# Layer 0 in half-blocks of f, late attention earlier, and two weight pairs decoded before the third block

## The chip, the cores and the metric

The kernel runs on one core of a Trainium2 chip. The metric is the device time of one execution in microseconds; lower is better. Five engines work side by side, each through a queue of its own: TensorE (PE, with its weight loads shown as PEld), VectorE (DVE), ScalarE (ACT), GpSimd (POOL) and SyncE (SP), which here issues the DMAs.

## The reference

Sliding-window attention with sink keys, then two feed-forward layers, all on 1536 tokens (2 batches of 768) of width 512:

```
scores = q @ k.T / sqrt(64)          # 8 heads of 64; keep key < 4, or 0 <= i - j < 128
x  = softmax(scores) @ v             # 1536 x 512
h  = x @ w_in                        # layer 0: 512 -> 2048
x  = (h * tanh(log(1 + exp(h)))) @ w_out      # 2048 -> 512
h  = x @ w2_in                       # layer 1
out = (h * clip(h + 3, 0, 6) / 6) @ w2_out
```

The weights arrive as 8-byte floating-point numbers.

## The kernel before

**Number format.** Every operand of a large matmul is split in two f16 parts, high and low, and a product is three matmuls (high by high, high by low, low by high). The weights are decoded on the chip: for each f, a slice of 128 of the 2048 hidden columns, SP loads two raw tiles of 512 KB (L166, L170) into one of two raw buffers, and `gen_decode` makes a 32-bit number of the two halves on DVE (L210 to L212) and splits it (ACT L222, DVE L224). Layer 1's weights are decoded in pairs of two f, because `split_pair` also forms sums and differences of the second matrix for a product with seven instead of eight multiplications (L249, L250, L260 to L268).

**Tokens.** 12 units of 128 tokens are in three blocks of four. The first eight units' attention (`First`, `first_blocks`) runs at the start. The last four (units 8 to 11, the third block) go through "late" attention: `gen_front` (keys and queries to f16, DMA transposes, scores on PE L551, minimum on DVE L558, exponent on ACT L565, split L578 and L581) and `gen_back` (values on PE L628 to L639, normalise L649, split and transpose into xt[2]). These generators yield 92 times; what lies between two yields is called a piece.

**Layer 0.** A step takes one block of 512 tokens and two f. `up` makes h with 24 matmuls of 512 columns (L737 to L739) and runs the activation: ACT L740 twice, L745, L746, L747; DVE L749 twice; ACT L753; DVE L754, which ends with the tile g. `down` multiplies g into four PSUM banks (24 matmuls, L782); it is written one step behind `up` (LAG = 1), so PE's order is up(s), down(s-1), up(s+1), down(s). There are 8 steps per block; before, the order of steps (STAGES) was all 16 f of block 0, then of block 1, then of block 2. After a block's last f, `finish` (L906, L907) takes the four banks into xt, the input of layer 1. With a span that ends before f = 16, `finish` copies the banks to SBUF on ACT instead (L897), and the later span adds them on DVE (L901).

**Layer 1** has half-blocks of 256 tokens and steps of four f (`up2`, `down2`, `finish2`).

**Side work.** `hook` is called four times a step, after each half of `up` and of `down`. At each call it takes RATES[stage] / 4 pieces of late attention and one half of a weight's decoding, the latter only up to a limit. Before, the limit was two or three f beyond what the steps so far needed (AHEAD) in the first two blocks; from the third block on it follows PAIRS, counted by step. `dec_side.until` decodes at once what the step itself needs. At the third block's first step `att_side.until` finishes late attention and `open_second` closes its buffers and opens, in their place, those for layer 1's weights.

**What sets the order.** The framework takes the instructions in the order written as their priority, and a planner with its own cost model lets each engine take the first one that it believes ready; so an instruction can stand earlier in its engine's queue than where it is written, if its data and its buffers are there. On the chip each queue then runs in the planned order.

Of the kernel before, what the change touches and what calls it, by code (L numbers as in the profile page):

```python
# [29 lines left out]
def attention_moe_moe2(  # L30
# [18 lines left out]
    KF = DFF // 128  # L49
# [21 lines left out]
    blocks = BLOCKS  # L71
    order = sum(blocks, [])
    first = blocks[0] + blocks[1]
    last = sum(blocks[2:], [])
# [81 lines left out]
    late = {}  # L156
# [312 lines left out]
    def open_second():  # L469

        p2.close()
        late["p"] = main.enter_context(tc.tile_pool(name="p_b", bufs=2))
        late["g7"] = main.enter_context(tc.tile_pool(name="g7", bufs=2 * (LAG + 1)))
        late["same"] = main.enter_context(tc.tile_pool(name="same", bufs=1))
        late["w_c"] = main.enter_context(tc.tile_pool(name="w_c", bufs=WC))
# [192 lines left out]
    def gen_units():  # L668
        assert all(u % NSB >= 2 for u in last)
        load_late(last[0])  # L670
        fr = {u: gen_front(u) for u in last}
        ahead = {u: 3 if u - 1 in last else 5 if u // NSB in {x // NSB for x in last[:n]} else 7 for n, u in enumerate(last)}
        yield from pieces(fr[last[0]], ahead[last[0]])
        for n, u in enumerate(last + [None]):
            if u is not None:
                yield from pieces(fr[u], 6)
            if n > 0:
                yield from gen_back(last[n - 1])
                yield ("unit", last[n - 1])
            if n + 1 < len(last):  # L680
                yield from pieces(fr[last[n + 1]], ahead[last[n + 1]])
            if u is not None:
                yield from pieces(fr[u], 7)
# [27 lines left out]
    att_side = Side(gen_units())  # L711
# [7 lines left out]
    def per_bank(blk):  # L719
        return 512 // (len(blocks[blk]) * 128)  # L720
# [109 lines left out]
    def down2(st, span):  # L830
        layer, blk, f = st
        g2 = gt.pop(st)
        fa, fb = span
        if f == fa:
            acc[layer, blk] = [ps_acc.tile([128, 2, 256], F32, tag="acc", name="acc") for _ in range(4)]
        a = acc[layer, blk]
        ends = f + 4 == fb
        turns = [(m, n) for m in range(2) for n in range(NP)]
        if ends:
            turns = [(m, n) for n in range(NP) for m in range(2)]  # L840
        for at, (m, n) in enumerate(turns):
            i = TURNS[n]
            g, w = g2[m][i], wt[1, 1, f // 2 + m][i]
            for x, (l_, r_) in enumerate(((g[:, 0], w[:, 0]), (g[:, 0], w[:, 1]), (g[:, 1], w[:, 0]))):

                nc.tensor.matmul(  # L846
                    a[n // 2][:, n % 2], l_, r_, start=f == fa and m == 0 and n % 2 == 0 and x == 0,
                    stop=ends and m == 1 and x == 2 and (n % 2 == 1 or n == NP - 1), skip_group_check=True,
                )
            if at % NP == NP - 1:  # L850
                hook()
        if f + 4 == fb:
            finish2(blk, {i: a[n // 2][:, n % 2] for n, i in enumerate(TURNS)}, span)
# [80 lines left out]

    steps = [((layer, j, f), (fa, fb)) for layer, j, fa, fb in STAGES for f in range(fa, fb, 2 * per_bank(j) if layer == 0 else 4)]
    budget = {"att": 0.0, "credit": 0.0, "lim": 0, "chk": False}
# [13 lines left out]

    def moe_steps():
        pend = []
        fmax = n2 = 0
        for s, (cur, span) in enumerate(steps):
            layer, j, f = cur
            fend = layer * KF + f + (2 * per_bank(j) if layer == 0 else 4)
            stage = STAGES.index((layer, j) + span)
            budget["chk"] = stage >= CHECK and not raw_t
            if f == span[0] and layer == 0 and j >= 2:
                att_side.until(("unit", blocks[j][-1]))  # L960
                open_second()
            budget["att"] = RATES[stage]
            if layer == 0 and j < 2:
                fmax = max(fmax, fend)
                budget["lim"] = 2 * min(fmax + AHEAD[stage], KF)
            else:

                budget["lim"] = 2 * (KF + 2 * PAIRS[n2])
                n2 += 1
            dec_side.until(("dec", fend - 1))  # L970
            (up if layer == 0 else up2)(cur)
            yield
            pend.append((cur, span))
            while len(pend) > LAG:
                x = pend.pop(0)
                (down if x[0][0] == 0 else down2)(*x)
        for x in pend:
            down2(*x)

    moe = moe_steps()  # L980
    first_blocks()
    p1.close()
# [187 lines left out]
NPART = 8  # L1170
TURNS = (0, 5, 4, 6, 2, 3, 1)
NATG = 2
STAGES = [(0, 0, 0, 16), (0, 1, 0, 16), (0, 2, 0, 16)]
STAGES += [(1, (j, h), fa, fa + 8) for fa in (0, 8) for j in (0, 1) for h in (0, 1)] + [(1, (2, h), 0, 16) for h in (0, 1)]
CHECK = 7
WC = 8
PAIRS = [1, 2, 3, 4, 4, 5, 6, 6, 7] + [8] * 100
LAG = 1
STB = 2
P1N = 8  # L1180
# [1 line left out]
P1V = 4  # L1182
P1D = 4
BLOCKS = [[6, 7, 0, 1], [2, 3, 4, 5], [8, 9, 10, 11]]
RATES = [2.5, 11] + [0] * 11
DPS = 1
AHEAD = [3, 2]


# [32 lines left out]
```

## Time and profile before

| | |
|---|---|
| median of 3 runs | 600.39 us (599.83 to 601.9) |
| the profiled execution | 599.53 us, span 597.7 us |
| PE busy | 579.0 us (97%) |
| DVE busy | 457.8 us (77%) |
| ACT busy | 398.4 us (67%) |
| granted TensorE clock, mean | 0.998 |

The span is the time from the first to the last instruction; the 1.8 us beyond it lie around it. An engine's idle time is the span less its busy time. The end of a matmul is modelled, so a short wait on PE shows a little smaller than it is. In the views, x is a count of instructions, and times are from the span's start.

Where the stages lie: block 0's first `up` starts at 72.4 us, beside the tail of the first attention; from 96.8 us layer 0 fills PE; block 1's first `up` starts at 161.3 us, block 2's at 264.5 us; layer 0's last `down` ends at about 361.6 us; layer 1 ends at 592.3 us.

### The profile page before, as it was taken

Reading aid. Unit: us, or ns where it says so; the run is one execution under the profiler, and the core shown is the slowest. Engines: PE = TensorE matmul, PEld = TensorE weight load, DVE = VectorE, ACT = ScalarE, POOL = GpSimd, SP = SyncE. Lnnn points to the kernel's source line nnn. Section 1 sums busy time; section 2 is a strip of 40 time slices with the busy share of each in tenths; the row PEclk is TensorE's granted clock in tenths of the full one; section 3 lists DMA queues with packets and bytes.
Section 4 is the critical chain, followed back from the end, with each engine's and each line's share of the span. In section 5 each row is a group of like instructions: output and inputs, shape, how many; then the busy total and the mean of one; then the engine's idle time right before and its main releaser. Section 6 shows DMA issues by size and latency. Waiting matters only on the chain.

```text
span 597.7 us, 11394 instructions
## 1 busy us (share of the span) xinstructions
PE 579.0 (97%) x4430; PEld 394.4 (66%) x4430; DVE 457.8 (77%) x1102; ACT 398.4 (67%) x786; POOL 24.8 (4%) x36
## 2 busy tenths in 40 slices
PE   7999999999999999899989999999999999999996
PEld 4778754444444545444434468888888888888885
DVE  5688998999365555489999999866687889874754
ACT  5998887777687776679888887434354656553532
POOL 0040010700000000000000000000000000000000
PEclk9999999999999999999999999999999999999999
DMA  9976357998334533254453442000007676400001
GB/s 179 226 163 212 101 183 199 230 261 213 96 73 74 80 60 73 47 159 141 157 192 122 163 143 71 1 1 2 1 7 249 215 263 223 142 34 1 36 1 39
DMA packets 105842, 72.24 MB, mean 121 GB/s; under 512 B 73512, under 2 KB 98088, under 8 KB 105784
## 3 DMA queue, kind: packets, MB, share of 16 engines
q1 hardware_dynamic: 105784, 71.48, 42.9%
q8 instruction: 35, 0.57, 0.4%
q14 instruction: 23, 0.19, 0.1%
HBM read 60.43 MB, written 3.15 MB: 106 GB/s over the span
## 4 chain that ended last, share of the span: by engine, by line
PE 59%; DVE 13%; ACT 12%; issue 11%; DMA 2%; POOL 2%; SPq 1%; DVEq 0%; ACTq 0%
PE acc L846 18%; PE h L806 7%; PE h L808 7%; PE h L807 7%; PE acc L782 6%; PE h L737 3%; PE h L739 2%; PE h L738 2%; DVE p L212 2%; ACT e L745 2%; ACT e L746 2%; DVE g L754 2%; ACT d L358 2%; ACT y L215 1%; PE o L393 1%
## 5 line engine op out<-in xcount | busy, mean ns | idle before, releaser
L782 PE MATMUL acc<-g,w 128*128 128x512 f16 x576 | 131.2, 379 | 5.4 <-DVE g L754 5.1
L846 PE MATMUL acc<-w,g 128*128 128x256 f16 x1008 | 113.8, 273 | 0.0
L846 PEld LDWEIGHTS <-g 128*128 128x128 f16 x1008 | 98.6, 98 | 11.4
L806 PE MATMUL h<-xt,w 128*128 128x256 f16 x384 | 104.7, 273 | 0.0
L808 PE MATMUL h<-xt,w 128*128 128x256 f16 x384 | 104.7, 273 | 0.0
L807 PE MATMUL h<-xt,w 128*128 128x256 f16 x384 | 104.7, 273 | 0.0
L782 PEld LDWEIGHTS <-w 128*128 128x128 f16 x576 | 55.3, 98 | 71.6 <-issue 7.0
L737 PE MATMUL h<-xt,w 128*128 128x512 f16 x192 | 72.8, 379 | 1.8 <-DVE mins L558 1.2
L739 PE MATMUL h<-xt,w 128*128 128x512 f16 x192 | 72.8, 379 | 0.0
L738 PE MATMUL h<-xt,w 128*128 128x512 f16 x192 | 72.8, 379 | 0.0
L810 ACT ACTIVATE e<-h,bias 128x512 f32<-128x512 f32 x48 | 32.5, 678 | 54.5 <-PE h L808 54.5
L811 DVE SCALAR_TENSOR_TENSOR e<-e,h 128x512 f32<-128x512 f32 x48 | 32.8, 684 | 41.8 <-ACT e L810 41.8
L823 ACT ACTIVATE g<-e 128x256 f16<-128x256 f32 x96 | 29.5, 354 | 28.8 <-DVE e L811 28.8
L823 ACT ACTIVATE g<-sm 128x512 f16<-128x512 f32 x48 | 30.2, 628 | 27.5 <-DVE sm L818 27.5
L749 DVE SCALAR_TENSOR_TENSOR e<-e,h 128x512 f32<-128x512 f32 x48 | 30.8, 683 | 16.5 <-ACT e L747 16.3
L824 DVE SCALAR_TENSOR_TENSOR g<-sm,g 128x512 f16<-128x512 f32 x48 | 33.1, 689 | 10.9 <-ACT g L823 10.8
L806 PEld LDWEIGHTS <-w 128*128 128x128 f16 x384 | 37.6, 98 | 4.6
L807 PEld LDWEIGHTS <-w 128*128 128x128 f16 x384 | 37.6, 98 | 4.5
L808 PEld LDWEIGHTS <-w 128*128 128x128 f16 x384 | 37.6, 98 | 4.3
L212 DVE SCALAR_TENSOR_TENSOR p<-raw,y 128x1024 int32<-128x1024 int32 x32 | 39.8, 1243 | 0.4
L740 ACT ACTIVATE e<-h 128x512 f32<-128x512 f32 x48 | 28.1, 588 | 16.4 <-PE h L739 16.4
L754 DVE SCALAR_TENSOR_TENSOR g<-e,g 128x1024 f16<-128x1024 f32 x24 | 29.4, 1226 | 8.3 <-ACT g L753 8.3
(172 smaller groups left out, 934.8 us busy)
## 6 DMA issues: line engine op xcount, KB each, us to landing
raw<-in_moe_w_in_dram SPq DMA_DIRECT2D x48, 512.0 KB, 4.2
raw<-in_moe_w_out_dram SPq DMA_DIRECT2D x48, 512.0 KB, 5.0
out_dram<-ob SPq DMA_DIRECT2D x12, 256.0 KB, 2.5
first<-in_k_dram SPq DMA_DIRECT2D x8, 256.0 KB, 4.8
first<-in_q_dram SPq DMA_DIRECT2D x8, 256.0 KB, 4.9
first<-in_v_dram SPq DMA_DIRECT2D x8, 256.0 KB, 3.1
nk<-in_k_dram SPq DMA_DIRECT2D x5, 256.0 KB, 5.1
nv<-in_v_dram SPq DMA_DIRECT2D x5, 256.0 KB
```

Source lines behind the costliest of these rows:

```text
L212: nc.vector.scalar_tensor_tensor(out=p, in0=t[:, :, 1], scalar=3, in1=y, op0=ALU.logical_shift_left, op1=ALU.bitwise_xor)
L737: nc.tensor.matmul(o, wh, x[:, 0, c, :], start=c == 0, stop=False)
L738: nc.tensor.matmul(o, wh, x[:, 1, c, :], start=False, stop=False)
L739: nc.tensor.matmul(o, wl, x[:, 0, c, :], start=False, stop=c == KD - 1)
L754: nc.vector.scalar_tensor_tensor(out=gl, in0=e, scalar=sc, in1=gh, op0=ALU.mult, op1=ALU.subtract)
L782: nc.tensor.matmul(o, l_, r_, start=first and m == 0 and x == 0, stop=last and end and x == 2, skip_group_check=True)
L806: nc.tensor.matmul(o, wh, x[:, 0, c, :], start=c == 0, stop=False)
L807: nc.tensor.matmul(o, wh, x[:, 1, c, :], start=False, stop=False)
L808: nc.tensor.matmul(o, wl, x[:, 0, c, :], start=False, stop=c == KD - 1)
L823: nc.scalar.activation(out=g[:, 0, d_], in_=src, func=AF.Copy, scale=sc)
L824: nc.vector.scalar_tensor_tensor(out=g[:, 1, d_], in0=src, scalar=sc, in1=g[:, 0, d_], op0=ALU.mult, op1=ALU.subtract)
L846: nc.tensor.matmul(a[n // 2][:, n % 2], l_, r_, start=f == fa and m == 0 and n % 2 == 0 and x == 0, stop=ends and m == 1 and x == 2 and (n ...
```

## The change

Blocks 0 and 1 of layer 0 are done in halves of f: block 0 with f 0 to 7, block 1 with f 0 to 7, block 0 with f 8 to 15, block 1 with f 8 to 15, then block 2 as before. So there are 16 steps in the first two blocks as before, in another order, and two more stage borders. The decoding limit of layer 0 is a list by step (DECS): after four steps 9 f, then one f a step. The rate of late attention rises from 2.5 to 8 pieces a step in the first four steps and is 9.5 in the next eight (before: 11 from the ninth step on). `open_second` is called at the first step at whose beginning late attention is all written, not at the third block's first step; from then on PAIRS counts, and it has four more entries at the front (1, 1, 2, 2), then 2, 3, 3, 4, 4, 5, 6, 6 in the third block (before: 1, 2, 3, 4, 4, 5, 6, 6). CHECK moves with the two more stages and names the same stage as before.

```diff
     def moe_steps():
         pend = []
-        fmax = n2 = 0
+        n2 = 0
         for s, (cur, span) in enumerate(steps):
             layer, j, f = cur
             fend = layer * KF + f + (2 * per_bank(j) if layer == 0 else 4)
             stage = STAGES.index((layer, j) + span)
             budget["chk"] = stage >= CHECK and not raw_t
-            if f == span[0] and layer == 0 and j >= 2:
-                att_side.until(("unit", blocks[j][-1]))
+            unit = ("unit", last[-1])
+            if layer == 0 and j >= 2:
+                att_side.until(unit)
+            if "w_c" not in late and unit in att_side.done:
                 open_second()
             budget["att"] = RATES[stage]
-            if layer == 0 and j < 2:
-                fmax = max(fmax, fend)
-                budget["lim"] = 2 * min(fmax + AHEAD[stage], KF)
+            if "w_c" not in late:
+                budget["lim"] = 2 * DECS[s]
             else:
 
                 budget["lim"] = 2 * (KF + 2 * PAIRS[n2])
...
-STAGES = [(0, 0, 0, 16), (0, 1, 0, 16), (0, 2, 0, 16)]
+STAGES = [(0, j, fa, fa + 8) for fa in (0, 8) for j in (0, 1)] + [(0, 2, 0, 16)]
 STAGES += [(1, (j, h), fa, fa + 8) for fa in (0, 8) for j in (0, 1) for h in (0, 1)] + [(1, (2, h), 0, 16) for h in (0, 1)]
-CHECK = 7
+CHECK = 9
 WC = 8
-PAIRS = [1, 2, 3, 4, 4, 5, 6, 6, 7] + [8] * 100
+PAIRS = [1, 1, 2, 2, 2, 3, 3, 4, 4, 5, 6, 6, 7] + [8] * 100
...
-RATES = [2.5, 11] + [0] * 11
+RATES = [8, 9.5, 9.5, 14] + [0] * 11
 DPS = 1
-AHEAD = [3, 2]
+DECS = [4, 6, 8, 9, 10, 11, 12, 13, 14, 15, 16, 16, 16, 16, 16, 16]
```

## Rows read from the trace of the kernel before

**Rows 1.** The page, its first part: busy us (share of the span) and instructions.
```profile
PE 579.0 (97%) x4430; PEld 394.4 (66%) x4430; DVE 457.8 (77%) x1102; ACT 398.4 (67%) x786; POOL 24.8 (4%) x36
```

**Rows 2.** Busy time by stage: stretch, length, each engine's busy us, clock, DMA.
```profile
96.77:161.29 64.52, 62.97 (x311) 28.35 (x310) 52.24 (x77) 48.31 (x65) 11.53 (x11) 1.00 0.80 206
161.29:264.52 103.23, 99.75 (x762) 49.76 (x761) 59.41 (x133) 76.06 (x137) 0.30 (x1) 1.00 0.40 82
264.52:361.61 97.09, 94.16 (x458) 44.57 (x456) 92.56 (x148) 82.49 (x124) 0.00 (x0) 1.00 0.42 141
361.61:592.26 230.65, 230.65 (x2113) 206.55 (x2111) 172.32 (x479) 111.23 (x256) 0.00 (x0) 1.00 0.24 81
```

**Rows 3.** Waits of PE from 96 to 362 us: total us, times, longest.
```profile
PE acc L782 <- DVE g L754: 5.1, 6, 1.4
PE h L737 <- DVE mins L558: 1.2, 1, 1.2
PE o L628 <- DMA atg<-ag: 0.7, 1, 0.7
PE h L737 <- DVE e L749: 0.6, 1, 0.6
```

**Rows 4.** Groups by line and shape, the activation: count | busy us, mean ns.
```profile
L740 ACT ACTIVATE e<-h 128x512 f32<-128x512 f32 x48 | 28.1, 588 | 16.4 <-PE h L739 16.4
L745 ACT ACTIVATE e<-e,one 128x1024 f32<-128x1024 f32 x24 | 27.5, 1146 | 0.6
L747 ACT ACTIVATE e<-e 128x1024 f32<-128x1024 f32 x24 | 25.2, 1049 | 0.4
L749 DVE SCALAR_TENSOR_TENSOR e<-e,h 128x512 f32<-128x512 f32 x48 | 30.8, 683 | 16.5 <-ACT e L747 16.3
L754 DVE SCALAR_TENSOR_TENSOR g<-e,g 128x1024 f16<-128x1024 f32 x24 | 29.4, 1226 | 8.3 <-ACT g L753 8.3
```

**Rows 5.** The same view, decoding of the weights.
```profile
L210 DVE TENSOR_SCALAR y<-raw 128x1024 int16<-128x1024 int16 x32 | 24.3, 759 | 4.6 <-DMA raw<-in_moe_w_out_dram 2.5 <-ACT y L215 1.9
L212 DVE SCALAR_TENSOR_TENSOR p<-raw,y 128x1024 int32<-128x1024 int32 x32 | 39.8, 1243 | 0.4
L224 DVE SCALAR_TENSOR_TENSOR w<-p,w 128x1024 f16<-128x1024 f32 x16 | 19.7, 1230 | 0.7 <-ACT w L222 0.5
L250 DVE SCALAR_TENSOR_TENSOR w<-p,w 128x512 f16<-128x512 f32 x16 | 11.1, 692 | 0.8 <-ACT w L249 0.8
L261 DVE TENSOR_TENSOR t<-p,t 128x256 f32<-128x256 f32 x8 | 3.4, 430 | 0.1
L268 DVE SCALAR_TENSOR_TENSOR w<-t,w 128x1024 f16<-128x1024 f32 x8 | 9.8, 1228 | 1.6 <-ACT w L267 1.6
```

**Rows 6.** The same view, late attention.
```profile
L565 ACT ACTIVATE d<-d,mins 128x272 f32<-128x272 f32 x32 | 16.3, 510 | 9.4 <-DVE mins L558 9.4
L558 DVE CUSTOM_DVE_ANT_0 d<-s,m_all 128x272 f32<-128x272 f32 x32 | 12.6, 437 | 4.7 <-PE s L551 4.7
L503 DVE SCALAR_TENSOR_TENSOR k<-nk,k 128x512 f16<-128x512 f32 x5 | 3.4, 685 | 0.1
L502 ACT ACTIVATE k<-nk 128x512 f16<-128x512 f32 x5 | 3.1, 627 | 3.0 <-DMA nk<-in_k_dram 2.1 <-DMA kt<-k 0.7
```

**Rows 7.** The same view, a PSUM bank copied on ACT, one read on DVE.
```profile
L371 ACT ACTIVATE at<-tp 128x512 f32<-128x512 f32 x22 | 12.4, 596 | 0.7 <-PE tp L369 0.7
L413 DVE TENSOR_TENSOR xf<-o,rib 128x512 f32<-128x512 f32 x8 | 5.5, 689 | 4.9 <-PE o L393 3.8 <-ACT d L358 1.2
```

**Rows 8.** Busy time by step (columns as in Rows 2), three steps of block 0.
```profile
117.66:128.59 10.93, 10.93 (x62) 4.97 (x60) 10.16 (x15) 7.91 (x10) 0.05 (x1) 1.00 1.17 299
128.59:139.52 10.93, 10.93 (x62) 4.95 (x61) 9.77 (x17) 8.40 (x15) 0.00 (x0) 1.00 0.96 236
150.93:161.29 10.36, 10.36 (x50) 4.67 (x49) 3.42 (x5) 6.74 (x8) 0.00 (x0) 1.00 0.36 115
```

**Rows 9.** DVE's timeline at the end of late attention: start us, us, what.
```profile
252.19 0.68 DVE L649 TENSOR_TENSOR xf<-o,ri 128x512 f32<-128x512 f32 x1
252.91 1.22 DVE L212 SCALAR_TENSOR_TENSOR p<-raw,y 128x1024 int32<-128x1024 int32 x1
```

## The prediction

> **What bounds the kernel now.** I read the page's first part first: PE is busy for 579.0 of 597.7 us [rows 1], so 18.7 us is all that could be won without taking matmuls away, and the change takes none away. Then the busy time by stage, to see where those idle microseconds lie [rows 2]: 64.52 - 62.97 = 1.55 us in block 0 (from the point where layer 0 has PE to itself), 103.23 - 99.75 = 3.48 in block 1, 97.09 - 94.16 = 2.93 in block 2, and nothing in layer 1, where PE is busy for 230.65 of 230.65 us. The change reorders layer 0 and moves work inside it; of its idle time there are 7.96 us, 1.3% of the span, and the rest of the 18.7 us lies in the start and the very end. Next, who ends those waits [rows 3]: 5.1 us in six waits are `down` waiting for the tile g that DVE L754 makes last in a step's activation; two waits (0.6 and 1.2 us) are `up` waiting for a PSUM bank that DVE still reads (L749, L558); one (0.7 us) is the last unit's values waiting for a DMA transpose. So PE sets the time, and where it stops, DVE is late in eight waits out of nine. The loads of DVE tell why [rows 2]: busy for 52.24 of 64.52 us in block 0 (81%, although its last step needs only 3.42 of 10.36 us; two earlier ones are at 93% and 89% [rows 8]), 59.41 of 103.23 (58%) in block 1, 92.56 of 97.09 (95%) in block 2. The work is there, but badly spread: full, half empty, full.
>
> **The change part by part.** One step of layer 0 takes 10.36 us of PE when nothing else is on it [rows 8]. Its activation takes 2 x 0.683 + 1.226 = 2.6 us of DVE and 2 x 0.588 + 2 x 1.146 + 2 x 1.049 = 5.6 us of ACT (L746 is of L745's form, L753 of L747's) [rows 4]. To decode one f of layer 0 takes 2 x 0.759 + 1.243 + 1.230 = 4.0 us of DVE (L211 is like L210) and some 1.05 of ACT, one pass of L747's size [rows 4, 5]. A pair of layer 1 takes 2 x (2 x 0.759 + 1.243 + 0.692) + 5 x 0.43 + 1.228 + 0.692 = 11.0 us of DVE: L210 to L212 and L250 twice, four sums like L261, and the split L268 of 1024 columns, with one of 512 and one of 256 that I take at L250's and L261's prices [rows 5]. Late attention on DVE is 32 x 0.437 + 8 x 1.226 (L581, of L754's form) + 23 conversions x 0.685 = 39.6, some 42 us with its small instructions; on ACT 32 x 0.510 + 8 x 1.05 + 19 x 0.627 = 36.6, some 39 us with the small ones [rows 4, 6]. Over 92 pieces that is 0.46 us of DVE and 0.42 of ACT each. On PE: block 1's stretch has eight steps, 99.75 - 82.9 = 16.9 us more than the steps alone, for about 84 pieces [rows 2, 8], so 0.2 us a piece.
>
> *Steps 2 and 3 of block 0* (the first two lie in the tail of the first attention and decode the same as before). Before, each of steps 2 to 6 had 2 f and 2.5 pieces on DVE: 2.6 + 8.0 + 1.2 = 11.8 us against 10.9 of PE, five steps in a row, and DVE ran full [rows 8]; this is block 0's 1.55 us. After: step 2 has 2 f and 8 pieces, 2.6 + 8.0 + 3.7 = 14.3 against 10.4 + 1.6 = 12.0; step 3 one f, 10.3 against 12.0. One step of 2.3 us too much and then relief, in place of five of 0.9. I keep 0.8 us, half of what is there.
>
> *Steps 4 to 10* now hold one f and 9 to 10 pieces each: DVE 2.6 + 4.0 + 4.4 = 11.0, ACT 5.6 + 1.05 + 4.0 = 10.6, PE 10.4 + 1.9 = 12.3. Both helpers at about 90%, where block 1 before had DVE at 58% and ACT at 76.06 of 103.23 (74%) [rows 2]. The new border at step 4 adds four copies of a PSUM bank on ACT, 4 x 0.596 = 2.4 us, as does the one at step 8 [rows 7]. Before, the only border inside attention was the one from block 0 to 1, with the same four on ACT and four on DVE, and there stood the two waits for PSUM banks, 0.6 + 1.2 = 1.8 us [rows 3]. At none of the new borders does DVE take part while attention runs, and pieces come at 9.5 and not 11 a step: I take half, 0.9 us; the ends are 0 and one such pair of waits at each border, 3.6.
>
> *The tail of attention*, steps 10 and 11: the last unit has nothing behind it to fill the time in which its weights are transposed. Before that cost the 0.7 us of the DMA wait, and a wait for g of about the same length beside it [rows 3]; nothing in the change touches this. I keep 1.6 us.
>
> *Opening the second buffers.* 4 pieces in step 1, 8 in steps 2 and 3 each, and 38 in the four steps of each of the next two stages make 96 by step 11; 92 are needed. So `open_second` comes at step 12 and not 16. DVE then starts layer 1's decoding as soon as the last unit is normalised: before, L212 followed L649 by 0.7 us [rows 9], twelve microseconds ahead of where it is written. The same should happen some 35 to 40 us earlier. Steps 12 to 15 take two pairs, 22 us of DVE, beside 4 x 2.6 and the additions at step 12 (four of 0.689 and four of `finish`, 5.5 us [rows 7]): 38 of 41.4 us, with step 11 almost empty before them.
>
> *Block 2* loses these two pairs and gains at its head block 1's additions: 92.56 - 22 + 2.8 = 73 of some 95 us, 77% in place of 95% [rows 2]. Its 2.93 us of waits were DVE's; I leave 0.9, one wait, for the steps that still take a whole pair.
>
> *The added work as a whole* is eight copies (4.8 us of ACT) and eight additions (5.5 us of DVE) [rows 7]; I cost it at nothing, since PE works beside it; fully exposed it would be 10.3, and I take 0 as the nearer end because the one border seen cost 1.8 with eight such instructions. Freeing PSUM banks at a border can't gain, as layer 0 uses the same four banks. `down` matmuls don't change in number. On SP's queue the transposes of attention now stand between loads of raw weights, which block 1 had not; a transpose that waits for its data holds the loads behind it. With two raw buffers and one f a step a load has about a step's time (12 us) in reserve, so 0 here, at most the 2.5 us that DVE waited for raw tiles in three places before [rows 5].
>
> Sum of what is left: 0.8 + 0.9 + 1.6 + 0.9 = 4.2 us, in place of 7.96: 3.8 us less. From the profiled execution's 599.53 us this gives 595.7; the median of the runs shown lies 0.86 above it, so 596.6 us for a median.
>
> **A rule weighed.** The six waits for L754 are the last link of a chain that changes between ACT and DVE [rows 3, 4]. The Trainium skill says of this, on its page PSUM — Partial Sum Buffer, section Engine vs sequencer instructions, that the queues of ScalarE and VectorE are strictly first in, first out. By that rule a piece that the planner put ahead of the activation holds it for its whole length, at 90% load too; what it would make of steps 2 to 10 is the first rival below.
>
> **The rivals.** *The waits move* into steps 2 to 10. For it: there ACT and DVE are both at about 90%, while block 2 before had DVE at 95% and ACT at 85% and lost 2.93 us in eight steps [rows 2]; the same rate over nine steps is 3.3, with the tail's 1.6, step 2's 0.8, the borders' 0.9 and block 2's 0.9 together 7.5: 600 us, no change. Against: attention's deadline is step 16, so the planner can let pieces slip.
>
> *All that can go goes*: only the tail's 1.6 us stay, 6.4 less, 594.0 us. For it: two steps at 93% and 89% of DVE, with scores in them, had no wait on PE at all [rows 8]. Against: no stage with attention was free of waits.
>
> *Slower: PSUM runs out.* `up` takes two of the four banks, a round of scores two more, and both are freed by DVE (L749, L558). With DVE at 90% rather than 58% the release comes later; the point where it decides is a DVE queue more than half an `up`, 2.6 us, behind PE. Then each of the 16 rounds of scores costs what the cheaper of the two such waits did, 0.6 us: 9.6, less the 1.8 already paid, plus the 1.6 at the tail unchanged, while blocks 0 and 2 gain 0.75 + 2.0: 600.4 + 7.8 - 2.8 = 605.4 us. For it: both waits of the kind are there [rows 3]. Against: in the two steps at 117.66 and 128.59, with DVE at 93% and 89%, 24 score matmuls ran with no wait [rows 8]. The Trainium skill (Perfetto Trace Analysis, section Optimization Strategy) says that a gap repeating through a stretch can mean that the next tile finds no room in SBUF or PSUM; by that, two waits in 16 rounds speak against this rival so far.
>
> *It doesn't do what it says*: attention isn't written by step 12, because a piece was miscounted. Then block 2 keeps its pairs, and only block 0's 0.75 us is won against the borders' copies: 599.7 us. The count above has four pieces to spare.
>
> **How the numbers follow.** My forecast 0.50; the waits move 0.22; all goes 0.11; PSUM 0.14; not done 0.03. A difference under 0.3%, 1.8 us, can't be told from none in this measurement. Faster by more (under 598.6): all of the third, 0.45 of the forecast's 0.50, 0.04 of the second: 0.60. Slower by more (over 602.2): PSUM's 0.14 and 0.02 of the second: 0.16. The same: the remaining 0.24. The range goes from 593.0, a microsecond below the case in which all goes, to 601.8, which takes in the moved waits with the borders' upper end (600 + 1.8) and leaves PSUM out; the forecast's own range is 594.5 to 599.
>
> **What would show it.** Right: the first L212 of layer 1 at about 210 to 222 us; block 2's stretch with DVE near 77% and under 1.5 us of PE idle; layer 0's last `down` ending near 358 us, layer 1 unchanged at 230.7 us; PE idle in layer 0 near 4 us. Step 2's term is wrong if waits for L754 between 96 and 120 us exceed 1.6 us; the borders' if L782 waits for L897 or L737 for L558 more than 1 us there. The prediction as a whole is wrong if PE idle between step 2 and step 11 exceeds 6 us, whichever engine ends it, or if block 2 keeps its 2.9 us although its two pairs are gone.

## The result and the profile after

The changed kernel takes 607.65 us (median of four, 606.73 to 608.0) beside 600.11 for the kernel before (four, 599.47 to 601.9): a ratio of 1.0128, 95% interval 1.0115 to 1.0141. It is slower by 7.5 us, where I forecast 3.8 us faster; the time lies above the range. The profiled execution took 606.73 us (span 604.9).

The page's first part, where [rows 1] has before:

```profile
PE 580.8 (96%) x4430; PEld 394.6 (65%) x4430; DVE 461.3 (76%) x1110; ACT 401.8 (66%) x794; POOL 19.9 (3%) x36
```

The same instructions but for eight each on DVE and ACT. PE is busy 1.8 us longer and idle 5.4 us longer (604.9 - 580.8 = 24.1 in place of 18.7).

Next the stretches: from the point in step 2's `up` where layer 0 has PE to itself to block 2's first `up`, then block 2, then layer 1 (columns as in [rows 2]):

```profile
96.76:273.44 176.68, 165.11 (x1071) 78.21 (x1070) 132.75 (x246) 136.37 (x228) 6.96 (x12) 0.97 0.60 147
273.44:368.81 95.37, 93.62 (x458) 44.61 (x456) 75.42 (x118) 74.58 (x106) 0.00 (x0) 1.00 0.31 102
368.81:599.50 230.69, 230.69 (x2115) 206.60 (x2114) 171.82 (x480) 110.66 (x254) 0.00 (x0) 1.00 0.24 80
```

Before, the first stretch was 167.8 us long with 162.7 of PE (the first two rows of [rows 2] together). It has grown by 8.9: 11.57 - 5.03 = 6.5 us more idle, and 165.11 - 162.73 = 2.4 us more *busy* time for the same 1071 matmuls, with the granted clock at 0.97 in place of 1.00. Block 2 gained 1.7 us, layer 1 is unchanged; 8.9 - 1.7 is the whole difference of the spans, 7.2.

Who ends PE's waits from 96 to 375 us (total, times, longest), where [rows 3] has before:

```profile
PE s L551 <- DMA qt<-q: 4.1, 1, 4.1
PE h L737 <- DVE e L749: 4.0, 1, 4.0
PE acc L782 <- DVE g L754: 2.4, 3, 0.9
PE o L628 <- DMA atg<-ag: 2.1, 1, 2.1
PE s L551 <- DVE mins L558: 0.7, 1, 0.7
```

The waits for g that I wanted to shorten did shrink, from 5.1 to 2.4 us, and two of the three left stand in block 2. In their place are three waits that the kernel before did not have, or not at this length. I call them A (4.1), B (4.0) and C (2.1).

**A: the first scores come before their queries.** Rows of the timeline (start us, us, what, and in brackets the idle time before it and its end's cause):

```profile
101.86 0.67 DVE L529 SCALAR_TENSOR_TENSOR q<-nq,q 128x512 f16<-128x512 f32 x1
102.44 2.33 SPq L601 DMA_DIRECT2D vsn<-in_v_dram  x4
105.38 1.31 SPq L505 DMA_TRANSPOSE kt<-k  x1
106.73 1.30 SPq L531 DMA_TRANSPOSE qt<-q  x1
110.74 1.54 PE L551 MATMUL s<-kt,qt 64*128 64x128 f16 x24 [4.12 <-DMA qt<-q]
```

The queries are split at 102.5, but SP is busy issuing the sink values, one more load and then the keys' transpose; the queries' transpose is issued at 106.7, and PE's first matmul on it starts 4.0 us later. With 8 pieces a step the planner put 24 score matmuls on PE ahead of step 3's `up`, and `up`, which had all it needed, stood behind them in PE's queue.

**B: an activation behind pieces.** Rows from the end of step 5's `up` to the start of step 6's; of ACT and DVE only what stands ahead of that activation (the others are left out):

```profile
142.54 0.63 ACT L502 ACTIVATE k<-nk 128x512 f16<-128x512 f32 x1 [0.74 <-DMA nk<-in_k_dram]
143.08 0.61 ACT L528 ACTIVATE q<-nq 128x512 f16<-128x512 f32 x1
143.60 1.04 ACT L222 ACTIVATE w<-p 128x1024 f16<-128x1024 f32 x1
144.55 0.57 ACT L740 ACTIVATE e<-h 128x512 f32<-128x512 f32 x1
145.03 0.61 ACT L510 ACTIVATE v<-nv 128x512 f16<-128x512 f32 x1
145.55 1.14 ACT L745 ACTIVATE e<-e,one 128x1024 f32<-128x1024 f32 x1
147.36 0.63 ACT L651 ACTIVATE x<-xf 128x512 f16<-128x512 f32 x1 [0.67 <-DVE xf L649]
147.89 1.13 ACT L746 ACTIVATE e<-e,fifth 128x1024 f32<-128x1024 f32 x1
149.06 1.06 ACT L747 ACTIVATE e<-e 128x1024 f32<-128x1024 f32 x1
151.38 0.74 DVE L210 TENSOR_SCALAR y<-raw 128x1024 int16<-128x1024 int16 x1 [1.08 <-DMA raw<-in_moe_w_out_dram]
152.01 1.27 DVE L749 SCALAR_TENSOR_TENSOR e<-e,h 128x512 f32<-128x512 f32 x2
152.74 0.58 PE L737 MATMUL h<-xt,w 128*128 128x512 f16 x1 [4.04 <-DVE e L749]
```

`up` of step 5 is finished at 142.5. Its second L740 then stands behind two conversions and a split of weights (2.0 us); L745 behind a conversion (0.5); L746 behind L651, which itself waits for DVE (1.2); and L749 behind a decoding instruction that waits for its raw tile (from 150.1 to 152.0: 1.9). That makes 5.6 us. By these rows the activation would without them have ended 4.6 us after its `up`, and PE had other work for 6.2 us (the value matmuls, `down` and 12 score matmuls): 1.6 of the 5.6 us are covered, 4.0 are the wait.

**The clock.** TensorE's granted clock behind A and B (columns as in [rows 2], the clock third from the right):

```profile
111.00:113.00 2.00, 2.00 (x26) 1.28 (x21) 1.38 (x5) 1.03 (x4) 1.19 (x3) 0.50 1.30 231
152.70:155.00 2.30, 2.26 (x6) 0.84 (x6) 2.30 (x5) 1.24 (x2) 0.00 (x0) 0.50 0.70 164
155.00:158.00 3.00, 3.00 (x10) 0.79 (x9) 1.93 (x4) 0.43 (x2) 0.00 (x0) 0.51 0.71 270
158.00:160.00 2.00, 2.00 (x21) 1.06 (x21) 1.49 (x5) 1.95 (x7) 0.00 (x0) 1.00 0.10 21
```

After each of these waits PE works at 0.50, the lower of its two levels (1.2 of 2.4 GHz), which no stretch of before showed [rows 2]. After B the first twelve `up` matmuls take from 152.74 to 157.95, 5.2 us, where twelve took 2.6 before; after A the 24 scores and three `up` matmuls take some 1.2 us more. These two make 3.8 us by the matmuls' starts, and the stretch's busy time grew by 2.4; where the 1.4 between were gained I did not trace.

**C and the end of attention:**

```profile
220.25 2.24 SPq L582 DMA_TRANSPOSE atg<-ag  x1
224.69 0.28 PE L628 MATMUL o<-vs,atg 128*128 128x256 f16 x1 [2.11 <-DMA atg<-ag]
226.25 0.69 DVE L649 TENSOR_TENSOR xf<-o,ri 128x512 f32<-128x512 f32 x1 [6.07 <-PE o L639]
226.98 1.23 DVE L212 SCALAR_TENSOR_TENSOR p<-raw,y 128x1024 int32<-128x1024 int32 x1
```

The last unit's attention weights take 4.4 us from the transpose's issue to PE's first matmul on them, and PE idles for 2.1 of them, with the rest of step 11's `up` planned behind that matmul. Layer 1's decoding begins 0.7 us after the last normalisation as before [rows 9], at 227.0.

### The profile page after: what moved, and what is told of

Read it like the earlier page. It is cut to its first block, busy times and chain, and to the rows that moved or that the text cites. A ratio compares the mean times of both kernels' runs of the same rounds, so it can differ in the third digit from the quotient of the medians.

```text
span 604.9 us, 11400 instructions
## 1 busy us (share of the span) xinstructions
PE 580.8 (96%) x4430; PEld 394.6 (65%) x4430; DVE 461.3 (76%) x1110; ACT 401.8 (66%) x794; POOL 19.9 (3%) x36
## 4 chain that ended last, share of the span: by engine, by line
PE 67%; DVE 14%; ACT 10%; DMA 4%; issue 3%; SPq 2%; POOL 0%; DVEq 0%; ACTq 0%
PE acc L846 18%; PE acc L782 10%; PE h L806 7%; PE h L807 7%; PE h L808 7%; PE h L737 4%; PE h L739 4%; PE h L738 4%; DVE g L754 2%; DVE p L212 2%; ACT d L358 1%; ACT e L745 1%; PE o L393 1%; ACT e L746 1%; DVE w L268 1%
## 5 line engine op out<-in xcount | busy, mean ns | idle before, releaser
L846 PE MATMUL acc<-w,g 128*128 128x256 f16 x1008 | 113.8, 273 | 0.0
L782 PEld LDWEIGHTS <-w 128*128 128x128 f16 x576 | 55.2, 98 | 68.4 <-issue 3.5
L737 PE MATMUL h<-xt,w 128*128 128x512 f16 x192 | 74.1, 386 | 4.0 <-DVE e L749 4.0
L738 PE MATMUL h<-xt,w 128*128 128x512 f16 x192 | 74.0, 386 | 0.0
L739 PE MATMUL h<-xt,w 128*128 128x512 f16 x192 | 74.0, 386 | 0.0
L740 ACT ACTIVATE e<-h 128x512 f32<-128x512 f32 x48 | 28.2, 587 | 27.1 <-PE h L739 26.6
L806 PEld LDWEIGHTS <-w 128*128 128x128 f16 x384 | 37.6, 98 | 4.6
L807 PEld LDWEIGHTS <-w 128*128 128x128 f16 x384 | 37.6, 98 | 4.6
L808 PEld LDWEIGHTS <-w 128*128 128x128 f16 x384 | 37.6, 98 | 4.3
L212 DVE SCALAR_TENSOR_TENSOR p<-raw,y 128x1024 int32<-128x1024 int32 x32 | 39.7, 1241 | 0.4
L749 DVE SCALAR_TENSOR_TENSOR e<-e,h 128x512 f32<-128x512 f32 x48 | 30.7, 679 | 9.1 <-ACT e L747 8.9
L738 PEld LDWEIGHTS <-w 128*128 128x128 f16 x192 | 19.0, 99 | 25.4 <-issue 5.1
```

What stands on the lines that cost most here:

```text
L212: nc.vector.scalar_tensor_tensor(out=p, in0=t[:, :, 1], scalar=3, in1=y, op0=ALU.logical_shift_left, op1=ALU.bitwise_xor)
L737: nc.tensor.matmul(o, wh, x[:, 0, c, :], start=c == 0, stop=False)
L738: nc.tensor.matmul(o, wh, x[:, 1, c, :], start=False, stop=False)
L739: nc.tensor.matmul(o, wl, x[:, 0, c, :], start=False, stop=c == KD - 1)
L782: nc.tensor.matmul(o, l_, r_, start=first and m == 0 and x == 0, stop=last and end and x == 2, skip_group_check=True)
L806: nc.tensor.matmul(o, wh, x[:, 0, c, :], start=c == 0, stop=False)
```

## The experiments

After the result my theory (T) was that A, B and C are the loss, and that they come from late attention's higher rate in the first steps, beside decoding. The rival H: doing the blocks in halves costs by itself, through the borders. A later rival, R, put B down to attention and decoding together on ACT and DVE, and T2 to the raw tile for which L210 waits in B. Each run is timed against the kernel before on the same chip, with the interval of the ratio in brackets; the change itself is at 1.0128, and its waits A, B and C come from one traced execution, as do those of every run.

**e1, late attention slow at the start:**

```diff
-RATES = [8, 9.5, 9.5, 14] + [0] * 11
+RATES = [2.5, 11, 11, 14] + [0] * 11
```

> The changed kernel with late attention at 2.5 pieces a step in its first stage (as before the change) and 11 in the next two, so that it still ends by step 12; halves of f, decoding pace and the early opening of layer 1's buffers stay. Theory T (the loss is made by waits of PE for DMA-fed instructions that the denser first half brings: 4.1 us for the transpose of the first queries at 106.6 us, 4.0 us at 148.7 us, each followed by microseconds at half the clock): the first scores come only about step 4, their transpose has landed, the 4.1 us wait and the 1.2 us of half clock behind it go, 602 to 603 us; 597 to 598 if the second wait goes too because the order is planned anew. Theory R (ACT and DVE carry too much in steps 2 to 10, so waits come wherever attention is dense): 11 pieces a step in steps 4 to 11 are denser still, the waits move there, 607 to 610 us. Theory H (the borders of the halves cost it): no change, 607.6 us.

602.63 us (1.0031 [1.0015, 1.0047]), as T had it: some three quarters of the loss by the ratio are gone. (Four of the ten executions took 600.4 to 601.1 us at a mean clock of 0.997 to 1.000, six 602.4 to 603.3 at 0.994 to 0.996.) A is gone with its half clock; B is 2.4 and 0.9 us in two places, without a drop; C is there, with a half clock behind it (two of the kinds of waits):

```profile
PE h L737 <- DVE e L749: 3.3, 2, 2.4
PE o L628 <- DMA atg<-ag: 2.5, 1, 2.5
```

**e2, the halves alone:** decoding, attention and opening as before.

```diff
+RATES = [2.5, 2.5, 11, 11] + [0] * 11
+DECS = [5, 7, 9, 11, 13, 15] + [16] * 10
-            if "w_c" not in late and unit in att_side.done:
+            if "w_c" not in late and layer == 0 and j >= 2:
+PAIRS = [1, 2, 3, 4, 4, 5, 6, 6, 7] + [8] * 100
```

> The kernel before with one part of the change alone: blocks 0 and 1 in halves of f. Late attention at 2.5 pieces a step in the first eight steps and 11 in the next eight, decoding up to 5, 7, 9, 11, 13, 15, 16 f by step, second buffers opened at the third block's first step and layer 1's pairs from there, all as before the change. Theory T: the halves by themselves cost nothing, 599 to 601 us. Theory H: most of the 7.5 us stays, 605 to 608 us, with waits of PE at the two new borders. Theory R: near 600 us, since the loads of steps 2 to 10 are those of before.

600.77 us (1.0012 [1.0001, 1.0023]). H falls as I put it: order and borders alone cost 0.7 us by the ratio, and the trace has that at the tail: C at 2.2 us with a half clock behind it. The first stretch is 1.9 us longer than before, block 2 0.2 shorter. What the halves add once attention is dense, no run shows: none has the early attention in the old order of blocks.

**e4, opening where before had it** (the last two edits of e2 alone):

> The changed kernel with the second buffers opened only at the third block's first step and the pairs counted from there, as before the change; late attention as in the changed kernel. All theories: steps 2 to 11 stay as in the changed kernel (the same waits of 4.1, 4.0 and 2.1 us, unless the order is planned anew). What it tells is the price of the other part: in the trace of the change PE idles 1.8 us from 273 us on and 0.6 in the half-block before, where before it idled 2.9 us in the third block. If the early opening is worth what that says, this run is 0.5 to 1.5 us slower than the changed kernel, 608 to 609 us; if the early opening itself costs time, it is faster, under 606.5 us.

608.09 us (1.0144 [1.0117, 1.0171]). That lies in the range that I gave for a working opening, but by luck: it is not to be told from the change, and block 2 takes 95.3 us as in the changed kernel. DVE's timeline tells why:

```profile
227.55 1.25 DVE L212 SCALAR_TENSOR_TENSOR p<-raw,y 128x1024 int32<-128x1024 int32 x1
```

Layer 1's decoding begins at the same place although it is written four steps later: the planner has it right behind the last unit's normalisation. So the written opening is worth nothing that can be measured here. That attention ends 26 us earlier lets three pairs instead of one be decoded ahead of block 2; whether this is what shortens block 2, run e13 below puts in doubt.

**e6, the sink values' loads later in SP's queue:**

```diff
-                yield from gen_sinks(b)
+                sinks = gen_sinks(b)
+                next(sinks)
+                yield
...
+        if sinks is not None:
+            yield from sinks
```

> The changed kernel with one piece written later: the four small loads of the sink values and what hangs on them come after the first queries' transpose, not before it. In the changed kernel SP issues them at 102.4 to 104.8 us, with the queries ready at 102.5 us and their transpose issued at 106.7 us. Theory T: the transpose is issued some 2.3 us earlier, the 4.1 us wait of PE shrinks to 2 us or less, the clock stays whole behind it; 2 to 4 us faster, 603.5 to 605.5 us, if the second wait stays. Theory R and theory H: no change, 607.6 us, the wait taken over by another instruction.

606.99 us (1.0117 [1.0087, 1.0147]), not to be told from the change: a miss by 1.5 us. A shrinks to 2.4 us and waits for the keys' transpose, but the clock does drop behind it (0.54 from 110.2 to 113.8 us), against theory T; B is 3.3 and 1.0. C is 2.1 as in the changed kernel, but here the clock drops behind it (0.66 from 222 to 227 us).

**e8, the first scores five empty pieces later:**

```diff
+        if u == last[0]:
+            yield from [None] * 5
```

with the two counts that go with it (`pieces(fr[u], 6 + 5 * (u == last[0]))`, third rate 10 made of 9.5 in the third stage).

> The changed kernel with five empty pieces between the transpose of the first late queries and the first round of scores, so that PE's planned order has the first scores behind half of the next up and not before it (and 10 pieces a step in the third stage, to end by the same step). Theory T: the 4.1 us wait of PE for the first queries and the half clock behind it are gone, and nothing takes their place at that point; 4 to 5.5 us faster, 602 to 604 us, if the wait of 4.0 us later on stays. Theory R (ACT and DVE are too full in steps 2 to 10): the time moves to waits for L749 or L754 there, under 1.5 us faster, over 606 us.

605.54 us (1.0102 [1.0085, 1.0118]): a miss by 1.5 us. A is down to 0.9 and the clock stays up there, and no wait of B's length is left; but other waits came, 3.4 us in three waits for DVE's minimum and 1.1 for L751, and C is 2.9 with a half clock behind it (0.79 from 219 to 227 us):

```profile
PE s L553 <- DVE mins L560: 3.4, 3, 2.4
PE o L630 <- DMA atg<-ag: 2.9, 1, 2.9
```

**e3, layer 0's weights decoded as early as before:**

```diff
+DECS = [5, 7, 9, 11, 13, 15] + [16] * 10
```

> The changed kernel with the decoding limits of before (5, 7, 9, 11, 13, 15, 16 f by step), so that two f a step are decoded until all 16 are there; PE's planned order of matmuls is the same as in the changed kernel, matmul by matmul. It is about the wait at 148.7 us, where an up waits 4.0 us for a PSUM bank that DVE L749 is to free. There L749 stands behind a decoding that waits for a raw tile until 151.4 us, and its ACT chain behind pieces of attention. Theory T2 (the raw tile is the cause: its load was issued late on SP behind attention's transposes): with two f a step in these steps more raw tiles are asked for beside the transposes, so waits for raw tiles grow, 608 to 611 us. Theory R (the load on ACT and DVE is the cause): two f a step beside 8 to 9.5 pieces overfill DVE in steps 2 to 6, 608 to 612 us as well, but then with DVE busy and not waiting for DMA before L749; if the time falls under 606 us, neither holds.

609.23 us (1.0161 [1.0136, 1.0185]). PE's planned order is the same as the changed kernel's. But the edit does not do what I expected of it: the decoding stands in the same steps as in the changed kernel (L212 six times in steps 3 to 6, none of layer 0 behind them), so "two f a step" was never tried, and the time in the expected range says little. What the run does show: B is 4.9 us although DVE waits for no raw tile there (1.1 us in the changed kernel). T2 falls: the raw tile was the last link, not the cause. Here a load of queries comes late instead, and ACT's queue stands behind it:

```profile
144.61 0.63 ACT L528 ACTIVATE q<-nq 128x512 f16<-128x512 f32 x1 [3.29 <-DMA nq<-in_q_dram]
```

So a late load in the queue of ACT or DVE can be part of B; what it holds up is everything planned behind it.

**e9, fewer pieces in the second stage** (`RATES = [8, 7, 12, 14]`):

> The changed kernel with late attention at 7 instead of 9.5 pieces a step in its second stage (steps 4 to 7, where the wait of 4.0 us at 148.7 us is) and at 12 in the third (steps 8 to 11, where decoding is nearly done and DVE is under half busy). Theory R (pieces ahead of the activation in the queues of ACT and DVE): the wait at 148.7 us goes, with the 2.6 us of half clock behind it, 600.5 to 603 us with the first wait still there. Theory T2 (the late raw tile alone): it shrinks only by the pieces' share, to 2 or 3 us; 604.5 to 606.5 us. Theory H: 607.6 us.

607.32 us (1.0126 [1.0109, 1.0143]): a miss by 4 us. A stays (3.5), C is 2.4 with a half clock behind it, and in place of B there are these, at 161 and 164 us, at half clock again (0.52 from 161 to 168 us):

```profile
PE s L551 <- DVE mins L558: 2.1, 1, 2.1
PE h L737 <- DVE e L749: 1.4, 1, 1.4
```

**e7, raw tiles issued by POOL**, which frees SP's queue (one of the two loads, its line shortened; the other is changed alike):

```diff
-        nc.sync.dma_start(out=t[:, 1]...
+        nc.gpsimd.dma_start(out=t[:, 1]...
```

> The changed kernel with the loads of the raw weights issued by POOL instead of SP (for all of layer 0 and 1), so that they don't stand in one queue with attention's loads and transposes; PE's planned order is the same but for the very first round of scores. Theory T2: SP is then free earlier for the first queries' transpose and the raw tiles are asked for on time, so both waits of 4 us shrink; the second one by the 1.1 us of DVE's wait for a raw tile and the 0.6 us of decoding behind it. 601 to 605 us, if POOL's own issuing is not slower than SP's. Theory R: the first wait may shrink, the second one stays over 3 us; 604 to 607 us. Issuing on POOL has a price of its own that no run here has shown: if loads take longer from there, decoding waits more, and the time rises.

644.49 us (1.0759 [1.0728, 1.079]), outside every range. Inconclusive for the question: the wait on the queries' transpose grew to 9.8 us, the longest for L749 is still 4.0, and POOL's queue, where each load waits for a free raw buffer, held other work of POOL back. Of the traced execution's 33.8 us, 20.6 are lost before the first stretch and 12.9 in it (189.59 us); what exactly cost them I did not pursue.

**e12, no decoding of f 8 to 15 in layer 0** (their decoded tiles are those of f 0 to 7; the loads and instructions go; the lines that skip the loads and reorder layer 1's buffers are not shown):

```diff
+        if layer == 0 and f >= KF // 2:
+            wt[0, 0, f], wt[0, 1, f] = wt[0, 0, f - KF // 2], wt[0, 1, f - KF // 2]
+            yield
+            return
```

> The changed kernel without the decoding of layer 0's f 8 to 15: their raw tiles are not loaded and the weights of f 0 to 7 are used again in their place, so part of the computation is replaced; attention, halves, borders and the first eight decodings stay, and layer 1's pairs take layer 0's unused buffers first. Steps 4 to 10 then hold attention without decoding. Theory R (attention and decoding together fill ACT and DVE, and their pieces stand ahead of the activation): the wait of 4.0 us at 148.7 us and the half clock behind it go, about 6.5 us, 600 to 602 us, and what stays is the wait for the first queries' transpose and the last unit's. If attention alone does it at 9.5 pieces a step: 605 to 608 us.

600.25 us (1.0007 [0.9998, 1.0016]), 7.4 less than the change and within what was expected. B and its half clock are gone, A and C are as they were:

```profile
PE s L557 <- DMA qt<-q: 4.0, 1, 4.0
PE o L634 <- DMA atg<-ag: 2.1, 1, 2.1
```

B needs both kinds of side work; with attention alone at the same rate there is none. That is R. The 7.4 us are more than B and its half clock (6.6), since the edit takes some 32 us of DVE's work away as well.

**e10, e1's slow start and three empty pieces ahead of the last unit's values:**

```diff
+RATES = [3, 11, 11, 14] + [0] * 11
+            if u is None:
+                yield from [None] * 3
```

> As the run with the slow start (3 pieces a step in the first stage, 11 in the next two), and three empty pieces before the last unit's values, so that PE's planned order has half a down and an up between the last two value rounds and the transposes they wait for. The slow start alone took 602.6 us, with a wait of 2.5 us for the last transpose and 3.4 us at half the clock behind it. Theory T for the tail (PE is sent to the last values before their transpose lands, 4.4 us after its issue): both go, 4 us, 598 to 599.5 us, and the run is faster than the changed kernel by 8 to 9 us and about as fast as or faster than the one before. If the wait for the values only moves to the next instruction: 601 to 603 us.

603.27 us (1.0061 [1.0044, 1.0077]): a miss by 4 us. C is still 1.6, and two other waits, 1.57 us up to 123 and 2.13 up to 161 us, each brought a half clock. That the two edits would add up was wrong (the rate is 3 here and was 2.5 in e1, so the order is another one already by that); why these waits come at these places I did not settle.

**e11, e2 with the same three empty pieces; e13, the kernel before with them:**

> As the run with the halves alone (600.8 us), and three empty pieces before the last unit's values. Its tail had a wait of 2.2 us and 3.4 us at half the clock. Theory T for the tail: both go, 3.5 to 4 us, 596.5 to 597.5 us, faster than the kernel before by 0.4 to 0.5%. If not the transpose but the end of attention as such costs it: 600 to 601 us.

> The kernel before, with nothing of the change, and three empty pieces before the last unit's values. Its tail idled 0.9 us before L782 and 0.7 us for the transpose, with the clock whole. Theory T for the tail: the 0.7 us goes, perhaps the 0.9 as well, 598.3 to 599.3 us; it also tells how much of the run with halves and tail is the tail's alone.

596.89 us (0.9946 [0.9934, 0.9958]), as expected, and 597.41 us (0.9956 [0.9944, 0.9968]), 0.9 us better than expected: both beat both kernels, and can't be told apart. PE's waits of e11, then of e13 (the two largest kinds), have none for atg any more, and the clock stays at 1.00:

```profile
PE acc L784 <- DVE g L756: 4.1, 5, 1.1
PE h L739 <- DVE mins L558: 1.1, 2, 0.9
```

```profile
PE acc L784 <- DVE g L756: 3.9, 6, 1.1
PE h L739 <- DVE mins L558: 1.4, 2, 1.2
```

So three empty pieces win 2.3 us (e13 against before) and 3.4 us (e11 against e2) by the spans. But not all of that is the tail. e13's first stretch and its block 2:

```profile
96.69:264.29 167.60, 162.70 (x1070) 78.31 (x1069) 109.92 (x205) 122.50 (x199) 12.24 (x12) 1.00 0.54 126
264.29:359.36 95.07, 93.99 (x458) 44.56 (x456) 91.37 (x149) 82.06 (x122) 0.00 (x0) 1.00 0.41 140
```

The first stretch, with the tail in it, is only 0.2 us shorter than before's 167.75, although the 0.7 us wait is gone; 2.0 of the 2.3 us are won in block 2, where DVE is as full as before (91.4 us against 92.6), attention ends 3 us later than before (255.2 against 252.2) and one pair is decoded ahead, as before. In e11 the first stretch is 3.2 us shorter than in e2 (166.55 against 169.71), where e2's C of 2.2 and its half clock stood, and block 2 0.9. So block 2's waits change with the planned order at the same load; which difference of order did it in e13 I did not find.

**e14, A, B and C taken away together:** e12 with e8's and e10's empty pieces (`RATES = [8, 10, 10.25, 14]`); like e12 it uses the tiles of f 0 to 7 twice.

> Like e12 (decoding of f 8 to 15 in layer 0 left out, the decoded tiles of f 0 to 7 used in their place), and besides: the first scores stand five empty pieces later, so that the three first up units come before them, and three empty pieces stand ahead of the last unit's values. Additive account (the three waits are the whole loss): e12's 600.25 less its wait on the queries' transpose 3.95, less some 1.2 for the half clock behind it, less its tail wait 2.1 gives 593 to 595; the stretch from 96.76 to the third block's first up is 162 to 164 long, with under 3 idle and no half clock. Rival (each replanning moves the waits, as in e8, e9 and e10): a new wait of over 1.5 in the dense stretch or at the tail, 597 to 600.

598.40 us (0.9966 [0.9955, 0.9977]). A, B and C are gone with every half clock, and the first stretch is 167.9 us long, as long as before's to 0.1 us. But it isn't the 593 to 595 that the plain account gives: new waits stand there. The time lies in the rival's range, though without the wait of over 1.5 us that it named; none is over 1.1 us:

```profile
PE s L559 <- DVE e L759: 1.3, 2, 1.0
PE s L559 <- DMA qt<-q: 1.1, 1, 1.1
```

Without the three waits the loss is gone; but they don't come off without smaller ones in their place. And since e14, like e12, leaves eight decodings out, it does not show by itself that the three waits are the whole loss.

## Why the prediction was wrong

The steps that failed are two terms of the sum, one cost taken at nothing, and the place where I took the decoding to stand.

*"Steps 2 and 3", 0.8 us, and "On SP's queue ... 0 here, at most the 2.5 us":* measured 4.1 us in A and some 1.2 of half clock behind it. I had weighed DVE's load and the raw loads' reserve. What decided was the front of the pipeline: the first unit's keys, queries and sink values all pass SP in a row, and the rate of 8 put their scores ahead of an `up` that was ready. e1 (slower start) takes A away, e8 (scores later) all but 0.9 us of it, e6 shortens it through SP's queue: A's mechanism is shown. My own signs for these terms (waits for L754 before 120 us, for L897 or L558 at the borders) did not show: A is a wait for a DMA, which none of them covers.

*"Steps 4 to 10", 0.9 us:* measured 4.0 us in B and some 2.6 of half clock. I costed the borders and the loads, with one f a step and DVE and ACT at "about 90%". The borders were right, nearly nothing (e2). The decoding does not stand where I had it. L212, once for each f decoded, in steps 3 to 6 and 7 to 11, first in the changed kernel, then before (us, busy us and count, clock, DMA):

```profile
112.22:167.32 55.10, 7.34 (x6) 0.93 1.00 235
167.32:231.23 63.91, 1.23 (x1) 1.00 0.33 72
```

```profile
106.48:150.93 44.45, 7.34 (x6) 1.00 0.96 240
150.93:213.69 62.76, 0.00 (x0) 1.00 0.41 81
```

The one behind step 6 is layer 1's. So layer 0's decoding ended with step 6 as before, whatever DECS says, and the change put late attention on top of the same six f instead of thinning them out. (That steps 2 to 6 held two f each before was wrong too: [rows 8] show less DVE work than my sum.) DVE's hole stayed in steps 7 to 11, and step 5, where B begins, was full:

```profile
136.45:152.74 16.29, 12.25 (x105) 6.28 (x101) 14.67 (x21) 13.27 (x22) 0.00 (x0) 0.95 1.19 267
167.32:231.23 63.91, 61.10 (x471) 30.40 (x469) 32.30 (x68) 44.53 (x77) 0.00 (x0) 1.00 0.33 72
```

There DVE is at 90% and ACT at 81%, in steps 7 to 11 at 51% and 70%. Before, two steps were as full on DVE (93% and 89%, with ACT at 72% and 77%) without a wait [rows 8], so such a load alone does not give the 4.0 us. The order does: five side pieces and one late raw tile stood between one step's `up` and its L749, in queues that ACT and DVE take as planned. The rule that I weighed said this (the Trainium skill, PSUM — Partial Sum Buffer, section Engine vs sequencer instructions: the queues of ScalarE and VectorE are strictly first in, first out). The trace agrees, with 5.6 us of L502, L528, L222, L510, L651 and L210 and their own waits ahead of one activation. I made it the first rival, at 600 us, by a rate of many small waits taken from block 2. The mechanism of that rival is what happened (e12 shows that it needs attention and decoding together); its price came out as one wait of 4 us, not nine of 0.4. How much of B each piece makes is read from one trace and not tested piece by piece.

*The clock stood in no term.* Before showed 1.00 in every stretch, and its longest wait was 1.4 us; I priced a longer wait at its length. A and B cost 3.8 us more for it by the matmuls' starts; net of what was gained elsewhere the stretch's busy time grew by 2.4.

*"The tail", 1.6 us:* 2.1. The step is sound, the size 0.5 short. That nothing in the change touches it was wrong: which matmuls the planner puts ahead of the last values and which behind differs from plan to plan (0.7 us before, 1.6 to 2.9 in the runs above, 0 in e11, e13 and e14).

*"Block 2", 0.9 us left:* 1.75, two waits of 0.88 in place of one; DVE at 75.4 of 95.4 us, 79% where I had 77%. The gain is there, but not by the written opening: *"Opening the second buffers"* at step 12 moves nothing (e4). Nor is it shown that the lighter load made it: e13 has a block 2 of 95.07 us, shorter than the change's, with DVE at 91.4 us (96%). My reading that block 2's 2.93 us came from DVE's 95% thus took a load for a cause. The first L212 came at 227.0, not 210 to 222: attention ended later than I had it, and A, B, C and the half clock, some 14 us, stand ahead of its end.

*The rivals.* "PSUM runs out" has the nearest time, 605.4, but not its mechanism: there is one long wait for L749 and one of 0.7 for L558, not sixteen of 0.6. The sign that I named for the whole was the right one: PE idle over 6 us between steps 2 and 11 was to show the prediction wrong, and it is 8.9 us to the end of step 10, 11.0 to the end of step 11.

What stays open: why e9 and e10 got their new waits where they did, what shortened block 2, whether early attention costs the same in the old order of blocks, and the 1.4 us that the first stretch won.

## What to carry to other kernels

Where side work is spread over a step, don't stop at each engine's load: write down, for the one activation that PE waits for, what the planned queues put between its inputs and its last instruction, and add these durations; here that gave 5.6 us in a step with DVE at 90% and ACT at 81%, a load that by itself had been priced at under 1 us. Look in the trace where side work that the source paces really stands: a limit that the planner passes by spreads nothing. When a pipeline is started earlier, follow its first item through the queue that issues its transfers and see what on PE stands behind it. And add to the price of a PE wait of some microseconds what the matmuls behind it may lose at half clock: here 1.2 us behind the 4.1 and 2.6 behind the 4.0.

## What the runs showed of the hardware

The clock does not follow the length of a wait alone. It was 0.50 after waits of 4.1 and 4.0 us here, and e10's drop at 123 us followed a wait of only 1.57; yet after C's 2.11 us it stayed at 1.00, as the row shows, while in e6, with the same order of matmuls on PE, the same wait of 2.11 brought 0.66 over the five microseconds around it (the second row):

```profile
224.60:227.00 2.40, 2.31 (x33) 1.58 (x34) 0.71 (x2) 1.07 (x2) 0.00 (x0) 1.00 0.02 7
```

```profile
222.00:227.00 5.00, 3.84 (x33) 2.39 (x34) 1.02 (x2) 1.66 (x3) 0.00 (x0) 0.66 0.13 26
```

In no traced execution did the clock drop between 96 and 375 us without a wait of over 1.5 us on PE shortly ahead; after waits of 2.35 (e8) and 2.37 us (e1) it stayed at 1.00. And the written place of the decoding was no place: four steps in the source (e4) were 0.6 us on the chip for layer 1, and the limit by step (e3) left layer 0's in the same steps.
